# Moving SyncE's closing waits from ahead of the last output store to ahead of the last three

## Chip, cores, metric

One core of a Trainium2 chip. The metric is the device time of one execution in microseconds (us). Every run told here is one that the measurement classes as fast, with a granted TensorE clock of 0.997 to 1.0 wherever the record lists it, so runs are compared as they stand.

## The reference

A layer normalisation, a sliding-window attention branch (32 heads of 18, window 256) and a gated feed-forward branch (4608 wide) on the same normalised input of 2048 x 576, joined at the end:

```python
xn = _layernorm(x, axis=-1)
s = _A_ref(xn, A_wqkv, A_wo)                              # attention
g = _silu(_B_ref(xn, B_w_gate, B_w_up, B_w_down))         # feed-forward
return x + s * g
```

Only the very end matters here: the last 128 rows of `x + s * g` are computed in two column pieces (352 and 224 columns) and stored.

## The kernel before

The kernel builds a graph of operations, schedules it on the five engines with its own model, and then writes each engine's instruction stream. A DMA raises a semaphore of its own "lane" by 16; whoever uses its data waits for that lane. The last chunk of the output goes out in these stores, all issued by SyncE (SP):

```python
# build_final, shortened: called with (c0=0, w=576) for most blocks of 128 rows,
# for the last one with (c0=0, w=352) and (c0=352, w=224)
q3 = op("DVE", ..., lambda e: e.tensor_tensor(xf, xf, t, ALU.add), f"fq3:{nm}", deps=[q2, o_dx], prio=2)
...
o = self.dma(self.out[rows, a:b], self.xf[:, sx, a:b], P * (b - a) * 2, f"dma:out:{sb}:{a}",
             ("out", sx if a == 0 else NFIN), deps=self.fq3, prio=2)
```

The instruction streams are written here. A `wait_ge` is an instruction of its own on the engine, or shares one with its neighbour:

```python
def run_engine(e, eng):
    known = {}
    for o in self.prog[e]:
        if e == "SP" and o is self.prog[e][-1]:           # ahead of SP's last operation, a store:
            for i, n in enumerate(lane_cnt):
                if n > 0 and i not in outs:
                    eng.wait_ge(lanes[i], n)              # one wait for every lane but the output lanes
        ...                                               # the operation's own waits
        ins = o.fn(eng)
        ...
    if e == "SP":
        for i in outs:
            eng.wait_ge(lanes[i], lane_cnt[i])            # the output lanes, behind the last store
        eng.nop()
```

The softmax here doesn't subtract the row's maximum and nothing guards it: scores larger than these inputs give would overflow.

## Time and profile before

| | before |
|---|---|
| time, median | 559.95 us (3 runs ahead of the prediction), 559.97 us (6 runs beside the change, the same 3 among them) |
| span of the profiled execution | 559.0 us |
| last matmul ends | 554.96 us |
| last vector sum (the output's last piece) ends | 556.39 us |
| last store starts | 557.35 us |

The table is read from the bottom up: between the last useful result and the store that carries it out lie 0.96 us, and from the store's start to the end of the span 1.65 us. The lines behind these numbers are in the prediction.

### The profile page before, as it was taken

What the parts mean: (1) busy time and instruction counts of PE and PEld (TensorE: products, weight loads), DVE (VectorE), ACT (ScalarE), POOL (GpSimd) and SP (SyncE); (2) the same over time, 40 slices, a digit from 0 to 9 for tenths busy, and PEclk for the clock granted to TensorE, in tenths of its full rate; (3) what the DMA queues carried; (4) which work ended last, traced back from release to release, by engine and by line L of the source; (5) the groups of instructions that cost most, each with busy time, mean ns of one, the idle gap of its engine ahead of it and who ended that gap; (6) DMA issues with size and microseconds to landing.
All of it is one profiled execution on the core that took longest, in us unless ns stands there. A gap on an engine that the chain in (4) does not pass through costs nothing.

```text
span 559.0 us, 19262 instructions
## 1 busy us (share of the span) xinstructions
PE 552.0 (99%) x8342; PEld 338.4 (61%) x8342; DVE 333.4 (60%) x797; ACT 274.2 (49%) x383; POOL 210.2 (38%) x360
## 2 busy tenths in 40 slices
PE   8999999999999999999999999999999999999997
PEld 7454444677755545467886555545688754444786
DVE  5477788787568667574558757357567623333033
ACT  4245654443656655645656464565756432323011
POOL 5464456566245454440667434034372200000000
PEclk9999999999999999999999999999999999999999
DMA  8977997831125534434121264245511035551010
GB/s 228 313 231 189 223 263 205 214 63 45 51 75 154 160 110 143 141 108 96 29 63 44 75 196 117 84 125 140 164 25 40 25 111 152 163 168 51 2 45 23
DMA packets 113468, 67.83 MB, mean 121 GB/s; under 512 B 18620, under 2 KB 111516, under 8 KB 113384
## 3 DMA queue, kind: packets, MB, share of 16 engines
q1 hardware_dynamic: 105960, 60.68, 39.4%
q0 software_dynamic: 7424, 5.92, 4.0%
q8 instruction: 66, 1.08, 0.8%
q14 instruction: 18, 0.15, 0.1%
HBM read 55.15 MB, written 2.36 MB: 103 GB/s over the span
## 4 chain that ended last, share of the span: by engine, by line
PE 98%; DMA 1%; SPq 1%; DVE 0%; issue 0%; DVEq 0%
PE ps L121 94%; PE ps L800 3%; DMA wgr<-in_B_w_up_dram 1%; SPq L278 1%; DVE s_attn L1061 0%; DVE thf L1066 0%; PE ps L598 0%; DVE xf L1071 0%; DVEq L1226 0%
## 5 line engine op out<-in xcount | busy, mean ns | idle before, releaser
L121 PE MATMUL ps<-xnT,wgs 64*128 64x512 bf16 (+1 forms) x2400 | 282.7, 368 | 0.7 <-DMA wgr<-in_B_w_up_dram 0.3
L750 ACT ACTIVATE expr<-ps 128x1024 bf16<-128x1024 f32 (+4 forms) x160 | 154.8, 969 | 77.8 <-PE ps L121 77.2
L121 PEld LDWEIGHTS ps<-xnT,wgs 64*128 64x128 bf16 x2400 | 113.8, 94 | 115.6 <-DVE hT L948 1.6
L121 PE MATMUL ps<-wd_sb,hT 64*128 64x288 bf16 (+2 forms) x2448 | 156.7, 276 | 0.0
L948 DVE SCALAR_TENSOR_TENSOR hT<-tring,ps 128x512 bf16<-128x512 bf16 x144 | 98.3, 683 | 95.0 <-ACT tring L945 93.9
L945 ACT ACTIVATE tring<-ps 128x512 bf16<-128x512 f32 x144 | 86.1, 598 | 130.0 <-PE ps L121 127.8
L121 PEld LDWEIGHTS ps<-wd_sb,hT 64*128 64x128 bf16 x2448 | 112.4, 94 | 28.5
L278 POOL DMA_DIRECT2D qk<-qd x160 | 82.2, 521 | 120.3 <-PE ps L121 109.7
L763 DVE TENSOR_TENSOR expr<-expr,mask 128x128 bf16<-128x128 bf16 (+2 forms) x240 | 63.4, 297 | 62.4 <-ACT expr L750 61.9
L714 POOL TENSOR_SCALAR kx<-kprev,small 128x256 bf16<-128x256 bf16 x64 | 61.3, 967 | 28.2 <-PE ps L121 27.4
L121 PE MATMUL ps<-qk,kx 64*128 64x320 bf16 (+1 forms) x704 | 59.4, 254 | 0.0
L278 POOL DMA_DIRECT2D oT<-o2T x72 | 36.4, 513 | 58.8 <-DVE o2T L826 49.8
L121 PE MATMUL ps<-xnT,wgr 64*128 64x512 bf16 (+1 forms) x300 | 55.9, 367 | 0.0
L121 PEld LDWEIGHTS ps<-qk,kx 64*128 64x128 bf16 x704 | 31.2, 94 | 21.6 <-ACT expr L750 0.6
L121 PE MATMUL ps<-xnT,wqk 64*128 64x512 bf16 x256 | 32.6, 376 | 0.0
L1051 ACT ACTIVATE thf<-ps 128x576 bf16<-128x576 f32 (+3 forms) x22 | 11.4, 518 | 39.7 <-PE ps L121 39.4
L818 DVE STREAM_TRANSPOSE ot<-ps 128x512 f32<-128x512 f32 x32 | 22.4, 699 | 11.6 <-PE ps L800 11.6
L714 DVE TENSOR_SCALAR kx<-qk,small 128x512 bf16<-128x512 bf16 x64 | 22.3, 378 | 4.7 <-PE ps L121 4.1
L121 PEld LDWEIGHTS ps<-xnT,wgr 64*128 64x128 bf16 x300 | 14.9, 94 | 16.5
L826 DVE STREAM_TRANSPOSE o2T<-o 128x512 bf16<-128x512 bf16 x32 | 22.7, 711 | 1.0
L636 DVE CAST qd<-ps 128x1024 bf16<-128x1024 f32 (+1 forms) x20 | 22.1, 1110 | 1.5 <-PE ps L121 1.5
L696 ACT ACTIVATE v_aug<-ps 64x288 bf16<-64x288 f32 x32 | 13.1, 408 | 17.3 <-PE ps L121 16.8
(71 smaller groups left out, 300.1 us busy)
## 6 DMA issues: line engine op xcount, KB each, us to landing
wgs<-in_B_w_gate_dram SPq DMA_DIRECT2D x72, 256.0 KB, 3.3
wgs<-in_B_w_up_dram SPq DMA_DIRECT2D x72, 256.0 KB, 3.8
wd_sb<-in_B_w_down_dram SPq DMA_DIRECT2D x9, 576.0 KB, 6.3
qk<-qd POOLq DMA_DIRECT2D x100, 36.0 KB, 2.4
wgr<-in_B_w_gate_dram SPq DMA_DIRECT2D x36, 64.0 KB, 2.2
wgr<-in_B_w_up_dram SPq DMA_DIRECT2D x36, 64.0 KB, 2.4
xf<-in_A_x_dram SPq DMA_DIRECT2D x16, 144.0 KB, 2.5
out_dram<-xf SPq DMA_DIRECT2D x15, 144.0 KB, 1.8
```

Source lines behind the costliest of these rows:

```text
L121: res = eng.matmul(outs[i], lhs(ROWS[t], i), rhs(ROWS[t], i), start=start, stop=stop, tile_position=(64 * t, 0))
L278: o = self.op(eng, DMA_ISSUE_NS[eng], lambda e: e.dma_start(dst, src), name, deps, prio, nbytes=nbytes)
L636: return eng.tensor_copy(dst, self.both(h, n))
L696: return eng.activation(dst, src, ACTF.Copy)
L714: return e.tensor_scalar(self.kx[:, sx, pos:pos + n_ // SW, t, :], src.rearrange("p (s k) -> p s k", k=SW), self.half[:, t:t + 1], None, A ...
L750: return eng.activation(self.expr[:, se, :, lo * SW:NT], self.both(h, NT)[:, :, lo * SW:NT], ACTF.Exp, scale=SM_SCALE)
L763: return eng.tensor_tensor(e_, e_, m_, ALU.mult)
L800: res = eng.matmul(outs[i][p0:p0 + VH, cols], self.v_aug[ROWS[i], o:o + VH], self.expr[ROWS[i], se, t, cols], start=n == 0, stop=n == len( ...
L818: return e.transpose(self.ot1[:, p1, :], self.halves(hp, NT)[i])
L826: t2 = op("DVE", dve_ns(NT), lambda e, p2=p2, p3=p3: e.transpose(self.o2T[:, p3, :], self.o2[:, p2, :]), f"ot2:{c}:{pr}:{i}", deps=[on, d3 ...
L945: th = op("ACT", act_ns(NT), lambda e: e.activation(self.tring[:, st, :], bank(h, 0), ACTF.Tanh, scale=0.5), f"th:{c}:{ft}", deps=[pg, dt_ ...
L948: mu = op("DVE", dve_ns(NT), lambda e: e.scalar_tensor_tensor(self.hT[:, ft, :], self.tring[:, st, :], 1.0, bank(h, 1), ALU.add, ALU.mult) ...
```

## The change

The lane waits at the end make sure that no DMA is still running when the program ends. They stood between the last two stores. The change puts them ahead of the third store from the end, where SP has nothing else to do.

```diff
+LAST_STORES = 3
...
-                if e == "SP" and o is self.prog[e][-1]:
+                if e == "SP" and o is self.prog[e][-LAST_STORES]:
                     for i, n in enumerate(lane_cnt):
                         if n > 0 and i not in outs:
                             eng.wait_ge(lanes[i], n)
```

## The prediction

> **What bounds the kernel now.** I read the page's header and chain first, to see whether there is any place where a change on SyncE (SP) can matter.
>
> ```profile
> span 559.0 us, 19262 instructions
> PE 98%; DMA 1%; SPq 1%; DVE 0%; issue 0%; DVEq 0%
> ```
>
> 98% of the chain that ended last is TensorE. The change touches no matmul, no vector instruction and no load, only the place of waits in SP's instruction stream. So it can act only where SP itself is on the path, and that is where the chain says "SPq" and "DMA": 1% each, in parts of one or two us. The place to look is the end, after the last matmul. The second view is therefore the instructions in order of time over the last 20 us (columns: start in us, length in us, engine, line, operation).
>
> ```profile
> 539.80 15.16 PE L121 MATMUL ps<-wd_sb,hT 64*128 64x288 bf16 x386
> 541.27 0.33 SPq L278 DMA_DIRECT2D xf<-in_A_x_dram  x1
> 550.58 0.46 DVE L1071 TENSOR_TENSOR xf<-xf,thf 128x576 bf16<-128x576 bf16 x1
> 551.06 6.62 SPq L278 DMA_DIRECT2D out_dram<-xf  x3
> 554.61 0.34 DVE L1071 TENSOR_TENSOR xf<-xf,thf 128x352 bf16<-128x352 bf16 x1
> 556.11 0.28 DVE L1071 TENSOR_TENSOR xf<-xf,thf 128x224 bf16<-128x224 bf16 x1
> ```
>
> The last matmul ends at 539.80 + 15.16 = 554.96. ScalarE and VectorE then work off the last 112-column half-blocks, and the last vector instruction, the sum that goes to the output, ends at 556.11 + 0.28 = 556.39. The span lasts until 559.0, so 2.6 us follow in which no compute engine does anything. The three last output stores are merged into one line here; asked for short stretches one by one, the same view gives two of their starts apart:
>
> ```profile
> 554.98 0.34 SPq L278 DMA_DIRECT2D out_dram<-xf  x1
> 557.35 0.33 SPq L278 DMA_DIRECT2D out_dram<-xf  x1
> ```
>
> Each store should start as soon as its vector sum ends. The first: sum ends 550.58 + 0.46 = 551.04, store starts 551.06, 0.02 later. The second: sum ends 554.61 + 0.34 = 554.95, store at 554.98, 0.03 later. The third: sum ends 556.39, store at 557.35, **0.96 us later**. Something else holds it. The views of the two source lines that emit waits, and of SP's own waits in the last 9 us, say what (for a source line: how often, duration in ns as least/median/most, first and last start):
>
> ```profile
> L1216 SPq EVENT_SEMAPHORE  x31: 27/28/28, 555.4 to 557.2; - x31
> L1226 SPq EVENT_SEMAPHORE  x1: 28/28/28, 557.3 to 557.3; - x1
> SPq L1232 <- DMA out_dram<-xf: 1.2, 1, 1.2
> ```
>
> L1216 is the closing wait on the lanes. Its 31 instructions run from 555.4 to 557.2, exactly between the second store and the third, and one more (L1226) follows at 557.3. They wait for nothing: the waits view lists no DMA as a releaser of line L278 in this stretch, and the lanes they ask for are all long satisfied. SP is merely executing them one after the other. Then the last store lands, and L1232, the wait on the store lanes, closes the program.
>
> **What the Trainium skill says.** "Advanced Engine Details and Errata", Network/Comms, puts reading a semaphore value from a sequencer at 50-100 ns on trn2. This trace agrees: from the end of the second store, 554.98 + 0.34 = 555.32, to the start of the third, 557.35, are 2.03 us with 32 wait instructions, 2.03 / 32 = 0.063 us each. "Perfetto Trace Analysis", Sequencer-only Instruction, says that the profiler shows only the execution of such an instruction and neither its decoding nor its wait. That fits too: the shown duration is 28 ns, the spacing 63 ns, so the sum of the durations (31 x 28 ns = 0.87 us) would understate the cost by more than half. The same page, DMA Instruction - HWDGE, has the decoding and the wait of a store ahead of its profiled start, on the issuing sequencer: a store that stands behind 32 waits in SP's stream cannot start before they are through, which is what 557.35 shows.
>
> **The change part by part.** It removes nothing and adds nothing. The lanes of the program, counted in the source, are 64 beside the three output lanes: 5 for x (4 for the first chunk, 1 for the later ones), 4 for wqk with its remainder, 3 for wv, 3 for wo, 8 for the gate and up weights and 4 for their remainders, 9 for the down weights, 8 for the transposing loads, 10 for qk, 8 for o, 2 for xf. With the store's own wait on VectorE that makes 65; at two to an instruction, 31 + 1 instructions take 64, and the store carries the last itself. The number of instructions thus checks with the trace, two waits to an instruction being my inference from it.
>
> What it moves: these waits from ahead of the last store to ahead of the third from the end, the one at 551.06.
>
> Step 1, cost at the new place. SP's last work before that store is the load of xf at 541.27, issued by 541.27 + 0.33 = 541.60. 32 instructions of 0.063 us end at 541.60 + 2.03 = 543.6. One of the lanes is that of the load just issued; its landing took 2.0 us in this trace (the median of all such loads is 2.5, by the page), so it lands at 543.3 to 543.8. SP then stands free at about 543.8, and the store's data are ready only at 551.04. That is 7.2 us of slack; the cost at the new place is zero. At most this first store's start slips by some 0.06 us, if its wait on VectorE now shares an instruction with the last lane. It has until 554.95, when the next one is due.
>
> Step 2, gain at the old place. After the second store SP is free at 555.32 and waits for VectorE alone, until 556.39. The third store then starts as the other two do, 0.02 to 0.03 us after its sum: 556.42. Gain: 557.35 - 556.42 = **0.93 us**.
>
> Step 3, the rest of the path. From the start of the third store to its landing were 1.5 us, and the wait at L1232 begins at 557.68 and takes 1.2, so it ends at 558.9; the span ends 0.1 later. All of this moves forward as it stands: the second store lands by 554.98 + 1.6 = 556.6, ahead of the third (556.42 + 1.5 = 557.9), so the third still decides the end. New span 559.0 - 0.93 = 558.1, new time 559.95 - 0.93 = **559.02 us**, 0.17% less.
>
> **The rivals.**
> (a) *All of the waits' time is won*: 559.95 - 2.03 = 557.9 us. Against it: 1.07 us of these waits (555.32 to 556.39) run beside ScalarE's and VectorE's last work. Only what stands out beyond 556.39 counts. 3%.
> (b) *The third store lands no sooner, or more slowly*, because it now comes 1.44 us after the second, not 2.37, and the two share the same 16 engines. By the DMA view, the second store's data move from about 555.7 to 556.3 and the third's from about 0.8 us after its start, which would be 557.2: they do not overlap. A landing of 1.8 us in place of 1.5, as the first, larger store had, would cost 0.3: 559.3 us. 10%.
> (c) *The moved waits block*: a lane that fills late would hold the first of the three stores. To cost anything at the end, SP would have to be held beyond 556.4, 15 us after the last load was issued, while the longest landing near by is 3.4 us. Even 64 separate waits would take only 4.0 us. GpSimd's last DMA is at 447, a hundred us earlier. Then the time would stay at 559.95 or rise; 2%.
> (d) *Nothing visible*, if the time outside the span (559.95 - 559.0 = 0.95 us) or a shift of the matmul stream absorbs the gain. The stream of TensorE is the same to the instruction and ends before SP matters, so I give it 3%, and some tenths of scatter.
>
> **Range and chances.** The three runs before lie within 0.23 us (559.84 to 560.07), a quarter of the gain, so the median should show it. Scatter of 0.1 to 0.2 on each side and rival (b) upward give 558.7 to 559.4. Faster by over 2% would take 11.2 us, where the whole tail after the last matmul is 4 us: out of reach. Slower by 2% would need a stall that nothing here can cause. Within 2%: 0.99.
>
> **What would show it.** In the changed kernel's trace: the 31 wait instructions start at about 541.6 and end at about 543.5; none stand between the second and the third store; the third store starts within 0.05 us of the last vector sum, at about 556.4; last matmul and last vector sum are where they were, within some tenths; store to landing still about 1.5 us; the span ends 2.6 - 0.93 = 1.7 us after the last vector sum. It would be wrong if the third store's gap to its sum stayed at several tenths (another instruction holds SP, such as a fetch), if its landing stretched, if the last matmul came later, or if the first store started visibly after 551.1 because a lane filled late.

## The result, and the profile after

The changed kernel took **559.03 us** (median of 6 runs, 558.70 to 559.24), beside 559.97 us (559.84 to 560.37) for the kernel before. The ratio is 0.9982, with a 95% interval of 0.9969 to 0.9995. It is the mean time of one kernel's fast runs over that of the other's of the same rounds, so not quite the ratio of the two medians. The median is lower by 0.94 us, and the interval lies clear of 1, but it is wide: it puts the gain anywhere between 0.3 and 1.7 us. The size of the gain must therefore be read from the traces.

The same views of the changed kernel, with line numbers one higher because of the added constant. First the instructions in order of time:

```profile
536.73 17.86 PE L122 MATMUL ps<-wd_sb,hT 64*128 64x288 bf16 x430
540.90 0.33 SPq L279 DMA_DIRECT2D xf<-in_A_x_dram  x1
550.20 0.46 DVE L1072 TENSOR_TENSOR xf<-xf,thf 128x576 bf16<-128x576 bf16 x1
550.75 5.62 SPq L279 DMA_DIRECT2D out_dram<-xf  x3
554.24 0.34 DVE L1072 TENSOR_TENSOR xf<-xf,thf 128x352 bf16<-128x352 bf16 x1
555.74 0.27 DVE L1072 TENSOR_TENSOR xf<-xf,thf 128x224 bf16<-128x224 bf16 x1
```

Asked in short stretches, the second and the third store:

```profile
554.61 0.34 SPq L279 DMA_DIRECT2D out_dram<-xf  x1
556.04 0.33 SPq L279 DMA_DIRECT2D out_dram<-xf  x1
```

The last sum ends at 555.74 + 0.27 = 556.01, the third store starts at 556.04. The gap of 0.96 us is now 0.03 us.

The closing waits, by their source line (count, duration in ns as least/median/most, first and last start):

```profile
L1217 SPq EVENT_SEMAPHORE  x31: 28/28/28, 541.3 to 543.9; - x31
```

And whom SP waited for in the stretch from 540 to 551 us (total us, times, longest):

```profile
SPq L1227 <- DVE xf L1072: 6.8, 1, 6.8
SPq L279 <- DMA out_dram<-xf: 1.4, 1, 1.4
SPq L1217 <- DMA xf<-in_A_x_dram: 0.8, 1, 0.8
```

The 31 wait instructions now run right behind the last load, from 541.3 to 543.9. One of them does wait in earnest, 0.8 us for the load just issued. Then SP stands idle for 6.8 us until the sum of the third store from the end. The waits have moved from a stretch in which SP is on the path into one in which it is not.

The two profiled spans differ by 559.0 - 557.7 = 1.3 us, more than the 0.94 us of the medians (the profiled run of the kernel before took 560.31 us, more than its median). Part of this is not the change: the last matmul ends at 536.73 + 17.86 = 554.59 here and at 554.96 before, 0.37 us earlier. So I compare the **tail**, from the end of the last vector sum to the end of the span: 559.0 - 556.39 = 2.61 us before, 557.7 - 556.01 = 1.69 us after. The tail is 0.92 us shorter. The views print a span to 0.1 us only, so a tail worked out from them is good to about 0.05 us. Read from the stored records without rounding, the two tails are 2.59 and 1.67 us, again 0.92 apart.

How far does the matmul stream scatter? The first of all output stores started at 145.5 us before and 145.1 after; over all nine profiled kernels it lies between 144.8 and 145.6, and the last matmul between 554.26 and 555.06. Before, 554.96 - 145.5 = 409.5; after, 554.59 - 145.1 = 409.5; in experiment 3, 554.26 - 144.8 = 409.5; by the stored records all nine lie between 409.48 and 409.50. In these profiled runs, whatever scatters does so in the first 145 us, far from the change.

### The profile page after: what moved, and what is told of

Read it like the earlier page. It is cut to its first block, busy times and chain, and to the rows that moved or that the text cites. A ratio compares the mean times of both kernels' runs of the same rounds, so it can differ in the third digit from the quotient of the medians.

```text
span 557.7 us, 19262 instructions
## 1 busy us (share of the span) xinstructions
PE 552.4 (99%) x8342; PEld 339.1 (61%) x8342; DVE 333.6 (60%) x797; ACT 274.3 (49%) x383; POOL 210.3 (38%) x360
## 4 chain that ended last, share of the span: by engine, by line
PE 98%; DVE 1%; DMA 0%; issue 0%; DVEq 0%
PE ps L122 95%; PE ps L801 3%; DMA x<-in_A_x_dram 0%; DVE small L525 0%; DVE small L527 0%; DVE xnr L541 0%; PE ps L599 0%; DVE s_attn L1062 0%; DVE thf L1067 0%; DVE xnr L545 0%; DVE small L529 0%; DVE small L531 0%; DVE xf L1072 0%; DVEq L1227 0%
```

## The experiments

**The theory:** SP executes these waits one after another at about 0.063 us per instruction of two, though they are already satisfied. They cost what of that execution stands out beyond the time at which the store behind them has its data, or, behind the last store, beyond its landing. **The rivals:** the waits cost in proportion to their number wherever they stand ahead of a store; the cost is one late lane or one instruction fetch and not the number; the gain is only the shifted matmul stream; the moved waits still cost something at the new place.

All seven kernels were correct. Each was run 5 times; experiments 1 to 4 share 9 runs of the kernel before (median 560.21 us), 5 to 7 share 9 others (560.27 us). The diffs of experiments 1 to 5 are written against the kernel before, those of 6 and 7 against the changed kernel. All seven were built from the changed kernel, so the constant is in them and their line numbers are those of its text or close to it. The table, read from the traces, gathers them; "gap" is from the last sum's end to the third store's start, "tail" from the last sum's end to the end of the span. (Unrounded, the tails are, from top to bottom: 2.59, 1.67, 1.73, 4.53, 1.67, 1.66, 2.46, 1.66 and 4.95 us.)

| kernel | last sum ends | third store starts | gap | span | tail | median us | ratio to before (95%) |
|---|---|---|---|---|---|---|---|
| before | 556.39 | 557.35 | 0.96 | 559.0 | 2.61 | 559.97 | |
| after | 556.01 | 556.04 | 0.03 | 557.7 | 1.69 | 559.03 | 0.9982 (0.9969 to 0.9995) |
| 1 half left | 556.36 | 556.45 | 0.09 | 558.1 | 1.74 | 558.91 | 0.9982 (0.9969 to 0.9994) |
| 2 twice, old place | 555.99 | 558.89 | 2.90 | 560.5 | 4.51 | 561.77 | 1.0033 (1.0020 to 1.0047) |
| 3 none | 555.69 | 555.72 | 0.03 | 557.4 | 1.71 | 558.95 | 0.9982 (0.9969 to 0.9994) |
| 4 ahead of two | 556.10 | 556.13 | 0.03 | 557.8 | 1.70 | 559.01 | 0.9983 (0.9970 to 0.9995) |
| 5 behind the last | 555.71 | 555.75 | 0.04 | 558.2 | 2.49 | 559.54 | 0.9989 (0.9975 to 1.0002) |
| 6 six times | 556.48 | 556.51 | 0.03 | 558.1 | 1.62 | 559.46 | 0.9989 (0.9976 to 1.0002) |
| 7 eight times | 556.45 | 559.66 | 3.21 | 561.4 | 4.95 | 562.09 | 1.0035 (1.0023 to 1.0048) |

### 1. Half of the waits left in the old place

```diff
-                if e == "SP" and o is self.prog[e][-1]:
-                    for i, n in enumerate(lane_cnt):
-                        if n > 0 and i not in outs:
-                            eng.wait_ge(lanes[i], n)
+                if e == "SP" and o in (self.prog[e][-LAST_STORES], self.prog[e][-1]):
+                    ks = [i for i, n in enumerate(lane_cnt) if n > 0 and i not in outs]
+                    for i in ks[:32] if o is self.prog[e][-LAST_STORES] else ks[32:]:
+                        eng.wait_ge(lanes[i], lane_cnt[i])
```

> 32 of the 64 lane waits stand ahead of the third store from the end, 32 stay between the last two. My theory (each wait instruction of two waits takes SP 0.063 us, and only what stands out beyond the last vector sum costs): 16 instructions after the second store end at 555.32 + 16 x 0.063 = 556.33, just ahead of the last sum at 556.39, so the third store starts 0.03 to 0.1 us after the sum and the time is that of the change, 559.0 to 559.1 us. Rival 1 (cost in proportion to the waits that stand there, no overlap with VectorE): half of the gain, 559.5 us. Rival 2 (the gain is not the waits but the matmul stream that happened to run earlier): time as before or as after, and the gap from sum to store stays near 0.9 us.

The third store of this kernel, and the wait lines on SP:

```profile
556.45 0.33 SPq L279 DMA_DIRECT2D out_dram<-xf  x1
```

```profile
L1217 SPq EVENT_SEMAPHORE  x30: 28/28/28, 541.6 to 556.2; - x30
L1227 SPq EVENT_SEMAPHORE  x6: 17/17/28, 182.1 to 556.4; - x6
```

The last lane wait of the old place starts at 556.2, just ahead of the sum's end at 556.36, and the gap is 0.09 us: 0.06 more than in the changed kernel. The line L1227 at 556.4 shows why: the store's own wait on VectorE now shares an instruction with the last lane, so one more instruction stands between the sum and the store. The time is 558.91 us; a cost in proportion to the number was put at 559.5 ahead of the run, which beside this set's own runs of the kernel before (560.21) would be about 559.7. The time alone does not rule it out, since the interval of the ratio (a gain of 0.3 to 1.7 us) holds half of the gain too; the gap does, with 0.09 us where half of 0.96 would be left. So all but 0.06 us of the cost is gone with half of the waits still in place: they run beside the vector work, as the prediction's account of the 1.07 hidden us has it.

### 2. The waits twice, in the old place

```diff
                 if e == "SP" and o is self.prog[e][-1]:
-                    for i, n in enumerate(lane_cnt):
-                        if n > 0 and i not in outs:
-                            eng.wait_ge(lanes[i], n)
+                    for k in range(2):
+                        for i, n in enumerate(lane_cnt):
+                            if n > 0 and i not in outs:
+                                eng.wait_ge(lanes[i], n)
```

> The 64 lane waits stand twice, in their old place between the last two stores. My theory: 64 instructions of 0.063 us from 555.32 end at 559.4, third store at about 559.4, time 559.95 + 2.0 = 562.0 us. Rival 1 (a satisfied lane costs only once, or the cost is one late lane or one instruction fetch, not the number): 560.0 us, or half of it at most.

The last sum, the third store and the waits:

```profile
555.72 0.27 DVE L1072 TENSOR_TENSOR xf<-xf,thf 128x224 bf16<-128x224 bf16 x1
558.89 0.33 SPq L279 DMA_DIRECT2D out_dram<-xf  x1
```

```profile
L1218 SPq EVENT_SEMAPHORE  x63: 27/28/28, 555.0 to 558.8; - x63
```

The second half of these waits asks for what the first half has just found satisfied, and still the third store starts 2.90 us after its sum in place of 0.96. The 32 added instructions cost 2.90 - 0.96 = 1.94 us, 0.061 us each. It is the number of instructions that costs, not a late lane or one instruction fetch: in the stored records of this kernel and of the kernel before, each of these waits but the first starts 59 to 75 ns after the one ahead of it, so no single long stop is hidden among them. The time, 561.77 us, was 562.0 in the expectation; the ratio 1.0033 over 560.21 is about 1.85 us.

### 3. No lane waits at all

```diff
-                if e == "SP" and o is self.prog[e][-1]:
-                    for i, n in enumerate(lane_cnt):
-                        if n > 0 and i not in outs:
-                            eng.wait_ge(lanes[i], n)
```

> No lane waits at all (every lane was waited for by its reader before, and the check finds no race). My theory: the moved waits cost nothing at their new place, so this equals the change: 559.0 us, third store 0.03 us after the last sum. Rival (the moved waits still cost something, through the first of the three stores or through SP): faster than the change by 0.1 us or more, 558.9 us or less.

The last sum and the third store:

```profile
555.41 0.28 DVE L1072 TENSOR_TENSOR xf<-xf,thf 128x224 bf16<-128x224 bf16 x1
555.72 0.33 SPq L279 DMA_DIRECT2D out_dram<-xf  x1
```

The tail is 1.71 us, with the change 1.69; the ratio is 0.9982 in both. At their new place the waits cost nothing that these runs can show. The times could not show a cost of 0.1 us, the rival's figure, for the five runs scatter from 558.62 to 559.65; the tails settle it, 1.67 us in both by the stored records. (By the expectation, the race check found nothing against leaving the waits out, since each lane has been waited for by its reader before; the results of this kernel were correct. The waits are a safeguard, and the change keeps it for free.)

### 4. Ahead of the last two stores

```diff
-                if e == "SP" and o is self.prog[e][-1]:
+                if e == "SP" and o is self.prog[e][-2]:
```

> The waits stand ahead of the last two stores (between the third and the second from the end). My theory: 2.03 us of waits from 551.40 end at 553.43, before the second sum at 554.95; equal to the change, 559.0 us. Rival (the place ahead of three stores is needed, since any wait between stores delays them): second store 0.5 us or more after its sum, time above 559.3 us.

```profile
L1217 SPq EVENT_SEMAPHORE  x31: 27/28/28, 551.2 to 553.0; - x31
```

They end at 553.0, ahead of the second piece's sum at 554.32 + 0.34 = 554.66; tail 1.70 us, time 559.01. Three stores are not needed; the shorter stretch of idle SP between these two stores holds the waits as well.

### 5. Behind the last store

```diff
                 # the lane waits ahead of the last store are taken out, and:
             if e == "SP":
+                for i, n in enumerate(lane_cnt):
+                    if n > 0 and i not in outs:
+                        eng.wait_ge(lanes[i], n)
                 for i in outs:
                     eng.wait_ge(lanes[i], lane_cnt[i])
```

> The lane waits stand behind the last store, ahead of the waits on the store lanes. My theory (SP executes them one by one, 0.063 us each): the third store starts at 556.42, SP is free at 556.75, 32 to 33 instructions end at 558.8, after the store has landed (557.9), so the end comes 0.8 us later than with the change: 559.8 to 559.9 us, nearly the time before. Rival (behind the store they are hidden in the landing): 559.0 us.

```profile
L1230 SPq EVENT_SEMAPHORE  x30: 17/28/28, 556.1 to 557.9; - x30
L1232 SPq EVENT_SEMAPHORE  x3: 28/28/28, 558.0 to 558.1; - x3
```

The third store starts at once (555.75) and lands after 1.5 us at about 557.3, but SP is at its waits until 558.1. The tail is 2.49 us, 0.80 longer than with the change, as expected: 1.2 us hide in the landing and 0.8 stand out. The time, 559.54 us, lies 0.3 below what I expected. In the profiled run that is the matmul stream, which ended at 554.29. By time alone this experiment would not be decided, since the interval of its ratio (0.9975 to 1.0002) holds both 1 and the 0.9982 of the change; the tail decides it.

### 6 and 7. Six and eight times, at the new place

```diff
                 if e == "SP" and o is self.prog[e][-LAST_STORES]:
-                    for i, n in enumerate(lane_cnt):
-                        if n > 0 and i not in outs:
-                            eng.wait_ge(lanes[i], n)
+                    for k in range(6):                    # experiment 7: range(8)
+                        for i, n in enumerate(lane_cnt):
+                            if n > 0 and i not in outs:
+                                eng.wait_ge(lanes[i], n)
```

> The 64 lane waits stand six times ahead of the third store from the end. My theory: 192 instructions of 0.063 us = 12.1 us, with 0.8 us for the landing of the last load, end at about 541.6 + 12.9 = 554.5; the first of the three stores starts 3.4 us late, the second just in time, the third unchanged: 559.0 to 559.1 us. Rival (waits ahead of the first store delay the end as they delay that store): 3 us more, about 562 us.

> The same eight times. My theory: 256 instructions = 16.1 us, with 0.8 us for the landing, end at about 558.5, beyond the last sum (556.39); the three stores then go out one after another at 558.5, 558.9 and 559.2, the last lands 1.5 to 1.8 us later, the span ends at about 561.0: 561.8 to 562.2 us. Rival (waits at this early place are free whatever their number): 559.0 us.

The first of the three stores and the last sum of experiment 6, by order of time, and its waits:

```profile
550.67 0.46 DVE L1072 TENSOR_TENSOR xf<-xf,thf 128x576 bf16<-128x576 bf16 x1
554.47 2.36 SPq L279 DMA_DIRECT2D out_dram<-xf  x3
556.21 0.27 DVE L1072 TENSOR_TENSOR xf<-xf,thf 128x224 bf16<-128x224 bf16 x1
```

```profile
L1218 SPq EVENT_SEMAPHORE  x191: 27/28/723, 541.8 to 554.3; - x191
```

The first store starts at 554.47, 3.34 us after its data were there (550.67 + 0.46 = 551.13), and the third still follows its sum by 0.03 us; the tail is 1.62 us. A store that is 3.3 us late costs nothing if it is not the last. The median, 559.46 us, missed the expected 559.0 to 559.1. The times, 558.84 to 559.47 and one of 560.99 us that stays unexplained, rule out the rival's 562 but are otherwise inconclusive: their interval holds both "as the change" and "as before". In the trace, two things differ without reaching the end: the second store took 0.76 us to issue in place of 0.34, and the first two landed after 2.2 and 2.1 us in place of the 1.8 and 1.7 of the changed kernel. That the stores came closer together does not explain it, since in experiment 7 they come closer still and land after 1.8 and 1.7 us; the cause stays open.

With eight times the waits, they reach beyond the last sum:

```profile
L1218 SPq EVENT_SEMAPHORE  x255: 27/28/837, 541.7 to 558.7; - x128
```

```profile
556.18 0.27 DVE L1072 TENSOR_TENSOR xf<-xf,thf 128x224 bf16<-128x224 bf16 x1
558.79 1.32 SPq L279 DMA_DIRECT2D out_dram<-xf  x3
```

From the end of the last load's issue (541.35 + 0.33 = 541.68) to the first store (558.79) are 17.11 us; without the 0.8 us of the one real wait, 16.3 us for 256 instructions, 0.064 us each. By the stored records this average holds two breaks of 0.3 us each in the row of waits (before 548.9 and 557.0), whose cause these runs do not show; without them it is 0.061, as in experiment 2. The three stores go out back to back, the third at 559.66, and the median of 562.09 us lies in the expected 561.8 to 562.2. So the new place is not free as such. It holds the waits because the slack there was larger than they are.

## Why the prediction was right

- **What bounds the end.** Said: the third store is held for 0.96 us by SP's own execution of satisfied waits. Experiment 2 shows it, since doubling the waits moved the store by 1.94 us, and experiment 3, since taking them away closed the gap to 0.03. One reading on the way there was wrong: the 1% each of SPq and DMA in the page's chain are not the end of the kernel. Followed in order of time, that chain has SP's eight load issues from 0.80 to 4.21 us and one weight load of 4.02 us behind them, and it ends with the last vector sum at 556.39. The place was found by the second view, not by these shares.
- **Cost of one instruction.** Said: 0.063 us. Measured: 0.061 (experiment 2) and 0.064 with two breaks, 0.061 without (experiment 7). The count of 31 + 1 instructions held in the changed kernel too, and the stored records name two semaphores on each of the 31, as was inferred.
- **Step 1, the new place.** Said: waits from about 541.6 to 543.5, SP free at about 543.8, no cost. The trace has 541.3 to 543.9, in a run whose load was issued 0.37 us earlier, with 0.8 us of waiting for that load's landing. The block thus ends some 0.5 us later than forecast, counted from the load. The prediction let the landing run wholly beside the waits; in the records the load's lane is asked for by the 17th of the 31 instructions, and the other 14 follow the landing at 543.0. It did no harm, since SP still stood idle for 6.8 us (7.2 forecast). No cost, by experiment 3. The slip of some 0.06 us of the first store came as described: 550.75 against a sum at 550.66, 0.09 us.
- **Step 2, the gain.** Said: 0.93 us, the part beyond the last sum, and not the 2.03 us of rival (a). The gap closed from 0.96 to 0.03 us, and the medians moved by 0.94. Experiment 1 shows that the remainder had been hidden: half of the waits in the old place cost only 0.06 us in the trace.
- **Step 3, the rest of the path.** Said: it moves forward as it stands, 1.7 us from the last sum to the end. Measured: 1.69, with the landing still 1.5 us. Rival (b), a slower landing because the stores come closer, did not occur. Even in experiment 7, with its stores at 558.79, 559.19 and 559.66, the third store landed after 1.6 us.
- **The range.** The time, 559.03 us, fell 0.01 from the predicted 559.02. That closeness is luck: the median of the unchanged kernel itself was 559.97, 560.21 and 560.27 us in the three sets. I took the scatter from three runs within 0.23 us; later sets of nine runs of the same kernel spread over 1.0 us (559.74 to 560.77, and 559.58 to 560.57). The range of 0.7 us was thus rather narrow, and it held partly by luck.

## What to carry to other kernels

A wait that is already satisfied still takes its turn in the issuing engine's stream (shown here for SP alone), so ask of every block of waits what stands behind it, and put safeguards where that engine is idle anyway. What such a block costs is neither its length nor its count but the part that stands out beyond the moment when the next instruction's data are ready. For a gain far below the scatter of whole runs, measure the stretch that the change touches, here from the last sum to the end, and let the traces decide.

## What the Trainium skill lacked or had wrong

- "Advanced Engine Details and Errata", Network/Comms, gives 50-100 ns for reading a semaphore value from a sequencer. The runs fit it, if a wait counts as such a reading, which the page does not say, and narrow it for SP: an instruction that waits for two satisfied semaphores takes 0.061 to 0.064 us of the stream, averaged over a block. The page does not say that satisfied waits add up like this: 32 instructions take 2.03 us.
- "Perfetto Trace Analysis", Sequencer-only Instruction, says that decoding and waiting are not in the profile, but not how much that hides: 28 ns shown against 63 ns spent here. For the waiting it is also not always so. In experiments 6 and 7 one instruction of the closing waits has a duration of 723 and 837 ns (the largest in their lines above). It names the last load's semaphore second, and it ends 22 ns after that load's landing. In the changed kernel the instruction that names this semaphore first shows 28 ns, and its 0.8 us of waiting lies ahead of its start.
- No page that I read has the time from issue to landing of small stores from SP. In the changed kernel it was 1.5 us for 56 KB, 1.7 for 88 KB and 1.8 for 144 KB.
- "DMA: Bandwidth & Descriptors", Specifications, has a first-byte latency of about 0.6 us for transfers issued by SP. Counted from the start shown in the profile, the data of the second and third store before and of the third after began to move about 0.8 us later (557.35 to 558.15 for the third before). The page does not say from which moment it counts, so this is a difference to keep in mind rather than an error.
